# Turning query tiles 4 to 6 through DRAM and VectorE, with query chains one slot shorter

## The chip, the cores and the metric

The kernel runs on one core of a Trainium2 chip. The metric is the device time of one execution in microseconds (us). Before the change three runs gave 856.16, 856.25 and 856.46, median 856.25. The execution whose profile is shown took 856.38, and its span, from the first to the last instruction, is 854.6.

The engines are TensorE (PE, matrix products; its weight loads are PEld), VectorE (DVE), ScalarE (ACT), GpSimd (POOL) and SyncE (SP). SP issues most of the DMAs; "SPq" is its queue. Each engine takes its instructions in the order in which the program gives them.

## The reference

Linear attention feeds two MLPs with different activations:

```
q_s = exp(q - max(q, axis=-1));  q_s /= sum(q_s, axis=-1) + 1e-9
k_s = exp(k - max(k, axis=2));   k_s /= sum(k_s, axis=2) + 1e-9
kv  = einsum('bhsd,bhse->bhde', k_s, v)
x   = einsum('bhsd,bhde->bhse', q_s, kv)        # as rows: 2304 x 512
x   = elu(x @ w_in) @ w_out                     # 512 -> 2048 -> 512
out = mish(x @ w2_in) @ w2_out                  # 512 -> 2048 -> 512
```

There are 4 batches, 8 heads, 576 positions, head size 64, all in fp32. The four weights arrive as 64-bit floats and are decoded on the chip.

## The kernel before

The 2304 rows are 18 query tiles of 128 rows. The ELU layer takes them in five groups j of 4, 3, 4, 3 and 4 tiles (tiles 0 to 3, 4 to 6, 7 to 10, 11 to 13, 14 to 17). For each group it goes through 16 slots f, one for each 128 columns of the hidden layer. All products are split into a high and a low part, so a slot has 12 products `mm_h(f)` into the hidden layer and 12 products `mm_y(f-2)` out of it, each with up to 512 columns. The Mish layer comes after that and takes the rest of the time.

While the slots of group j run, the kernel prepares group j+1: the keys and values of the next batch (`kv_chain`) and the query tiles (`q_chain`). The steps are put into the slots by `at(j, f, where, fn, ...)`, and in every slot the lists "pre", "load", "mid", "pe", "post", "last" and "late" are run in that order around the slot's own work. Nothing reorders them: the place in the text is the place in each engine's queue. The first five slots of group 0 are an exception, there the list FIRST gives the order by names, and x0, x1, ... are the steps that `at` put there.

A query tile is loaded (`load_q`, on SP), its maxima are taken over each head (`q_max`, DVE) and subtracted (`q_less`; POOL for tiles 4 to 6, DVE for later ones), ACT takes the exponential (`q_exp`), DVE sums (`q_sum`, with two small instructions for the inverse), and the tile is scaled (`q_norm`, POOL or DVE). Then it has to be turned, so that the head's columns lie on the partitions:

- Tiles 4 to 6 are turned by TensorE: `q_turn` has four 128x128 transposes into PSUM, and ACT copies the result back (`q_turned`).
- Tiles 7 to 17 go out to DRAM (`q_out`), come back in four DMAs with their 32x32 blocks at the places of the turned tile (`q_in`), and DVE turns each block in place (`q_blocks`, one instruction).

At the end `q_x` multiplies with the kv matrices on TensorE, ACT copies the high part (`x_hi`), and DVE subtracts it for the low part (`x_lo`). With f the slot of the exponential, `q_x` of tiles 4, 5 and 6 stands in slots 10, 12 and 14 of group 0.

The query tiles lie in a pool with two buffers (tag "q", tiles 4, 5, 6, 7, 8, 10, ... take them in turn), so the load of a tile waits until `q_x` of the tile two before has read its buffer. One tile in each later group (o == 2) lies in one of the three key buffers instead (`load_q3`).

In every slot of group 0 two 512 KB weight pieces are decoded: ACT (`rebias`, slot f-1), two instructions of `decode_low` and two of `decode_join` on DVE (slot f, "pre"), a copy of the high part on ACT (`piece_hi`, "mid") and the low part on POOL (`piece_lo`). The slot's own vector work is `elu_join(f)` and, a slot later, `split_lo(f)`, which writes the tile gl that `mm_y(f)` needs from its second product on. Pieces that are no longer in the early buffers go through four "raw" buffers.

Of the kernel before, what the change touches and what calls it, by code (L numbers as in the profile page):

```python
# [8 lines left out]
F32 = mybir.dt.float32  # L9
F32R = mybir.dt.float32r  # L10
U32 = mybir.dt.uint32
# [5 lines left out]
P = 128  # L17
# [15 lines left out]
    lo0 en1 li3 2i4 1o2 ee2 ej1 2o1 my0 x2 x3 en2 pi4 ld1 2o2 ej2 li4 gh1 mh3 x4 x5 gh2 x6 bo3  # L33
    x7 1o3 1i5 mh4 gl1 bi5 2i5 po1 2o3 bi6 po2 1i6 lo1 gl2 x8 ee3 x9 po3 x10 x11 2i6 ee4
    my1 1o4 bo4 en3 2o4 x12 x13 lo2 x14 pi5 ej3 lo3 en4 x15 li5 x16 ej4 gh3 my2 ld3 pi6 mh5 ld2
    po4 li6 x17 ld4 lo4 gl3 x18
""".split()


# [1 line left out]
def attention_elu_mish(  # L41
# [15 lines left out]
    nc = tc.nc  # L57
    B, DM, S = kT.shape
# [3 lines left out]
    NHP = DM // P  # L62
# [6 lines left out]
    TILES = (4, 3, 4, 3, 4)  # L69
    NA = len(TILES)  # L70
    assert sum(TILES) * P == NT
    at0 = [sum(TILES[:j]) for j in range(NA)]
# [8 lines left out]
    NC = (S + P - 1) // P  # L81
# [6 lines left out]
    dram = ctx.enter_context(tc.tile_pool(name="dram", bufs=1, space=bass.MemoryType.DRAM))  # L88
# [25 lines left out]
    stage = att.enter_context(tc.tile_pool(name="stage", bufs=2))  # L114

    raw = {}
    w_hi, w_lo, split_t = {}, {}, {}
    w_src = {("i", 0): w1_in, ("o", 0): w1_out, ("i", 1): w2_in, ("o", 1): w2_out}  # L120

    def load_piece(kind, layer, f, t=None):
        w = w_src[kind, layer]
        if t is None:
            t = stage.tile([P, 512, 2], U32, tag="raw", name="raw", bufs=4)
        c = slice(f * P, (f + 1) * P)
        if kind == "i":
            nc.sync.dma_start(
                out=t.rearrange("p (k c) two -> p k (c two)", c=P),
                in_=w[:, c, :].rearrange("(k p) c two -> p k (c two)", p=P),  # L130
            )
        else:
            nc.sync.dma_start(out=t, in_=w[c, :, :])
        raw[kind, layer, f] = t
# [67 lines left out]
    ap = att.enter_context(tc.tile_pool(name="att", bufs=2))  # L202
# [3 lines left out]
    km_t, qm_t, kv_t, turn_t, x_t = {}, {}, {}, {}, {}  # L206
    k_t, v_t, q_t, rk_t, en_t = {}, {}, {}, {}, {}
# [25 lines left out]
    def load_q(i, t=None):  # L233
        if t is None:
            t = ap.tile([P, DM], F32, tag="q", name="q")
        nc.sync.dma_start(out=t, in_=q[i * P:(i + 1) * P, :])
        q_t[i] = t
# [76 lines left out]

    R = 32

    def q_out(i):
        d = dram.tile([P, DM], F32, name=f"turn_q{i}")
        nc.sync.dma_start(out=d, in_=q_t[i])
        turn_t[i] = d  # L320

    def q_in(i):

        d = turn_t.pop(i).rearrange("(a j) (h r i) -> r j h a i", j=R, r=P // R, i=R)
        for r in range(P // R):
            nc.sync.dma_start(
                out=q_t[i][r * R:(r + 1) * R, :].rearrange("j (h a i) -> j h a i", h=NHP, i=R),
                in_=d[r],
            )

    def q_blocks(i):
        nc.vector.transpose(out=q_t[i], in_=q_t[i])

    NH = DM // D

# [1 line left out]
        return q_t[i].rearrange("p (h d) -> p h d", d=D)  # L337

    def load_q3(i):
        t = ap.tile([P, NC, P], F32, tag="kT", name="kT", bufs=3)  # L340
        load_q(i, t.rearrange("p c e -> p (c e)")[:, 0:DM])

    def q_max(i):
        m = sp.tile([P, NH], F32, tag="qm", name="qm")
# [264 lines left out]
    for n, t in enumerate(("xhb", "xlb")):  # L609
        t = xpool.tile([P, KD * TILES[1] * P], F32, tag=t, name="early_x")  # L610
        for hp in (2 * n, 2 * n + 1):
            a = hp % 2 * NC * P
# [4 lines left out]
    def at(j, f, where, fn, *a):  # L617
        j, f = j + f // NF, f % NF
        beside.setdefault((j, f, where), []).append((fn, a))
# [5 lines left out]
    def kv_chain(j, f, b):  # L625
        for hp in range(NHP):

            s = f + 2 * hp
            if j or hp > 2:
                at(j, s - 2, "load", load_k, b, hp)  # L630
            if (b, hp) not in v_t:
                at(j, s + 2, "load", load_v, b, hp)
            at(j, s, "late", k_max, b, hp)
            at(j, s, "late", k_exp, b, hp)
            at(j, s + 2, "post", lambda b, hp: inverse(rk_t[b, hp]), b, hp)
            at(j, s + 3, "post", k_scale, b, hp)


            rest = s + 1 if j else s + 2
            if j and hp:  # L640
                at(j, s + 1, "pe", k_kv, b, hp - 1)
            at(j, rest, "pe", k_turn_rest, b, hp)
            at(j, rest, "pe", k_turned_rest, b, hp)
            if not j or hp == NHP - 1:
                at(j, s + 3, "pe", k_kv, b, hp)
            at(j, s + 1, "pe", k_turn, b, hp)
            at(j, s + 1, "pe", k_turned, b, hp)

    def q_chain(j, f, i, o):
        at(j, f - 2, "late", load_q3 if j and o == 2 else load_q, i)  # L650
        at(j, f - 1, "late", q_max, i)
        at(j, f - 1, "late", q_less, i, NORM[j])
        at(j, f, "mid", q_exp, i)
        at(j, f, "late", q_sum, i)
        at(j, f, "late", q_norm, i, NORM[j])
        for fn in (q_x, x_hi, x_lo):
            at(j, f + (5 if j else 2), "pe", fn, i)
        if j:
            at(j, f + 1, "late", q_out, i)
            at(j, f + 2, "late", q_in, i)  # L660
            at(j, f + 4, "post", q_blocks, i)
            return
        for fn in (q_turn, q_turned):
            at(j, f + 1, "pe", fn, i)


    turns = {-1: [("i", 0, 0), ("i", 0, 1)]}
# [8 lines left out]
    for j in range(NA - 1):  # L676
        if j + 1 < B:
            kv_chain(j, -1 if j else 0, j + 1)
        for o in range(TILES[j + 1]):
            q_chain(j, 9 - 3 * (TILES[j + 1] - 1 - o) if j else 8 + 2 * o, at0[j + 1] + o, o)  # L680

    for n in range(NF):
        j, s = 1 + n // 4, n % 4 * 4
        for key, s in ((("i", 1, n), s), (("o", 1, n), s + 2)):
            at(j, s - 2, "load", load_piece, *key)
            at(j, s - 1, "last", rebias, key)
            at(j, s, "pre", decode, key)
            at(j, s + 1, "mid", split_piece, *key)
# [4 lines left out]
    with tc.manual_schedule():  # L693
# [14 lines left out]
        def load_turn(f, which=(0, 1)):  # L708
            for n in which:
                key = turns[f][n]  # L710
                n += (f + 1) % 4 * 2
                t = early[4 + n // 2].bitcast(U32)[:, n % 2 * 1024:(n % 2 + 1) * 1024]
                load_piece(*key, t.rearrange("p (c two) -> p c two", two=2))
# [4 lines left out]
        def load_ahead(f):  # L718
            if f + 3 < RING:
                load_turn(f + 3)  # L720
            else:
                while later and sum(key in raw for key in late) < 4:
                    key = later.pop(0)
                    late.append(key)
                    load_piece(*key)

        late = []
# [73 lines left out]
        for key in [key for f in range(-1, AHEAD) for key in turns[f]]:  # L801
            n = f"{key[0]}{key[2]}"
# [10 lines left out]
        n = 0  # L813
# [27 lines left out]
        for s in range(AHEAD, len(slots) + LAG1):  # L841
            if s < len(slots):
                j, f = slots[s]
# [18 lines left out]
            if s >= LAG1:  # L862
                j, f = slots[s - LAG1]
# [9 lines left out]
        for s in range(len(slots) + LAG2):  # L873
            if s < len(slots):
                p, f = slots[s]
# [6 lines left out]
            if s >= LAG2:  # L882
                p, f = slots[s - LAG2]
# [41 lines left out]
```

## Time and profile before

| | |
|---|---|
| median of 3 runs | 856.25 us (856.16 to 856.46) |
| profiled execution | 856.38 us, span 854.6 us |
| PE busy | 843.7 us (99%) |
| DVE busy | 599.4 us (70%) |
| ACT busy | 451.1 us (53%) |
| POOL busy | 160.3 us (19%) |
| granted TensorE clock | 0.999 of full speed |
| DMA | 104.05 MB |

Busy time is the share of the span in which an engine had an instruction in work. The products of TensorE overlap, so the length shown for one is longer than the distance to the next; where a text speaks of the pace, it takes the distance of two starts. In a timeline the number in brackets is the idle time ahead of an instruction and what ended it.

### The profile page before, as it was taken

The page shows a single profiled execution, that of the slowest core. Times are in us where ns is not written, and L with a number is a line of the kernel's source. Part 1 is how long each engine was busy: PE and PEld are TensorE (multiplying, and loading weights), DVE is VectorE, ACT ScalarE, POOL GpSimd, SP SyncE. Part 2 cuts the span into 40 slices and gives each one's busy share as a digit, 9 for nine tenths or more (in the row PEclk, how much of TensorE's full clock was granted, in tenths as well). Part 3 has the DMA queues.
Part 4 walks back from the last instruction along what each step waited for, and adds up shares of the span by engine and source line. Part 5 has one row for each costly group of instructions (what it writes and reads, how often), then busy time and mean ns, then how long its engine had stood idle before and what let it go on. Part 6 is the DMA issues. An engine that isn't in the chain of part 4 may idle for free.

```text
span 854.6 us, 11819 instructions
## 1 busy us (share of the span) xinstructions
PE 843.7 (99%) x4364; PEld 728.6 (85%) x4364; DVE 599.4 (70%) x1051; ACT 451.1 (53%) x854; POOL 160.3 (19%) x210
## 2 busy tenths in 40 slices
PE   7999999999999999999999999999999999999998
PEld 5778889998888899988889998888888888888996
DVE  7899866665555577554446877777787777777776
ACT  7797757656554465554444444444444444444443
POOL 4366523233212242223332000000000000000000
PEclk9999999999999999999999999999999999999999
DMA  9791648673845196538876003000210021000101
GB/s 302 251 306 55 197 129 279 182 231 98 232 131 161 52 265 196 166 99 286 278 243 227 1 0 103 34 1 0 99 50 1 0 74 50 1 1 1 50 1 37
DMA packets 79865, 104.05 MB, mean 122 GB/s; under 512 B 27328, under 2 KB 56256, under 8 KB 77248
## 3 DMA queue, kind: packets, MB, share of 16 engines
q1 hardware_dynamic: 63536, 58.08, 22.8%
q0 software_dynamic: 16128, 45.09, 16.0%
q8 instruction: 34, 0.56, 0.3%
q14 instruction: 23, 0.19, 0.1%
q10 hardware_dynamic: 144, 0.13, 0.0%
HBM read 73.14 MB, written 30.15 MB: 121 GB/s over the span
## 4 chain that ended last, share of the span: by engine, by line
PE 95%; ACT 1%; issue 1%; POOL 1%; DVE 1%; DMA 0%; SPq 0%; POOLq 0%; ACTq 0%
PE h L428 45%; PE y L477 23%; PE y L565 15%; PE a L565 8%; PE a L388 2%; PE a L297 1%; PE a L263 1%; DMA q<-in_q_dram 0%; POOL wil L186 0%; PE a L280 0%; DVE qs L359 0%; ACT early L148 0%; PE a L374 0%; ACT woh L180 0%; POOL wol L186 0%
## 5 line engine op out<-in xcount | busy, mean ns | idle before, releaser
L443 DVE SCALAR_TENSOR_TENSOR e<-h,e 128x512 f32<-128x512 f32 (+1 forms) x80 | 50.9, 636 | 106.7 <-ACT e L439 106.2
L428 PE MATMUL h<-xha,wih 128*128 128x512 f32 (+1 forms) x328 | 125.0, 385 | 0.7 <-ACT xha L404 0.7
L428 PE MATMUL h<-xla,wih 128*128 128x512 f32 (+1 forms) x328 | 125.2, 385 | 0.4 <-DVE xla L408 0.4
L428 PE MATMUL h<-xha,wil 128*128 128x512 f32 (+1 forms) x328 | 125.2, 385 | 0.3 <-POOL wil L186 0.3
L533 ACT ACTIVATE r<-n,two 128x512 f32<-128x512 f32 (+1 forms) x80 | 54.6, 682 | 131.1 <-DVE n L529 131.1
L477 PE MATMUL y<-gh,wol 128*128 128x512 f32 (+1 forms) x320 | 120.1, 377 | 0.3 <-POOL wol L186 0.3
L477 PE MATMUL y<-gh,woh 128*128 128x512 f32 (+1 forms) x320 | 117.4, 368 | 0.0
L477 PE MATMUL y<-gl,woh 128*128 128x512 f32 (+1 forms) x320 | 117.2, 368 | 0.0
L435 ACT ACTIVATE e<-h 128x512 f32<-128x512 f32 (+1 forms) x80 | 44.5, 556 | 115.9 <-PE h L428 115.8
L428 PE MATMUL h<-xhb,wih 128*128 128x384 f32 (+1 forms) x304 | 104.7, 344 | 0.0
L428 PE MATMUL h<-xhb,wil 128*128 128x384 f32 (+1 forms) x304 | 104.6, 344 | 0.0
L428 PE MATMUL h<-xlb,wih 128*128 128x384 f32 (+1 forms) x304 | 104.4, 344 | 0.0
L186 POOL TENSOR_TENSOR lo<-raw,hi 128x512 fp32r<-128x512 f32 x32 | 43.9, 1372 | 229.9 <-ACT hi L180 144.8
L512 ACT ACTIVATE u<-h 128x512 f32<-128x512 f32 (+1 forms) x80 | 44.1, 551 | 72.1 <-PE h L428 72.1
L522 DVE TENSOR_SCALAR u<-u 128x512 f32<-128x512 f32 (+1 forms) x80 | 32.0, 400 | 64.9 <-ACT u L512 63.6
L565 PE MATMUL y<-woh,gl 128*128 128x512 f32 x192 | 75.2, 392 | 0.0
L565 PE MATMUL y<-woh,gh 128*128 128x512 f32 x192 | 75.1, 391 | 0.0
L565 PE MATMUL y<-wol,gh 128*128 128x512 f32 x192 | 74.7, 389 | 0.0
L461 DVE TENSOR_TENSOR gl<-e,gh 128x512 fp32r<-128x512 f32 (+1 forms) x80 | 52.4, 656 | 28.6 <-ACT gh L457 28.5
L428 PEld LDWEIGHTS h<-xha,wih 128*128 128x128 f32 x328 | 61.1, 188 | 13.2 <-ACT xha L404 0.9
L428 PEld LDWEIGHTS h<-xha,wil 128*128 128x128 f32 x328 | 61.1, 188 | 12.9 <-POOL wil L186 0.9
L457 ACT ACTIVATE gh<-e 128x512 fp32r<-128x512 f32 (+1 forms) x80 | 47.0, 588 | 47.3 <-PE y L477 39.3
(163 smaller groups left out, 1755.8 us busy)
## 6 DMA issues: line engine op xcount, KB each, us to landing
raw<-in_moe_w_out_dram SPq DMA_DIRECT2D x23, 512.0 KB, 4.9
raw<-in_moe_w_in_dram SPq DMA_DIRECT2D x21, 512.0 KB, 5.2
early<-in_moe_w_in_dram SPq DMA_DIRECT2D x11, 512.0 KB, 6.3
early<-in_moe_w_out_dram SPq DMA_DIRECT2D x9, 512.0 KB, 6.5
out_dram<-o SPq DMA_DIRECT2D x17, 256.0 KB, 2.0
w2ih<-hi POOLq DMA_DIRECT2D x16, 256.0 KB, 2.7
w2il<-lo POOLq DMA_DIRECT2D x16, 256.0 KB, 3.8
w2oh<-hi POOLq DMA_DIRECT2D x16, 256.0 KB, 3.3
```

Of the source, the lines that this page charges most:

```text
L186: nc.gpsimd.tensor_tensor(out=lo, in0=z, in1=hi.bitcast(F32), op=ALU.subtract)
L388: nc.tensor.matmul(out=ps[:, hp, t0:t1], lhsT=kvbd[b % 2][:, hp, :], rhs=u[:, hp, t0:t1], start=True, stop=True,)
L428: nc.tensor.matmul(out=h_t[f][:, c], lhsT=w[:, i, k * P:(k + 1) * P], rhs=x[k][:, c], start=(n == 0), stop=(n == 3 * KD - 1),)
L435: nc.scalar.activation(out=e, in_=h_t[f], func=AF.Exp)
L443: nc.vector.scalar_tensor_tensor(out=e, in0=h_t[f], scalar=0.0, in1=e, op0=ALU.max, op1=ALU.subtract)
L457: nc.scalar.activation(out=gh_t[f], in_=h_t[f], func=AF.Copy)
L461: nc.vector.tensor_tensor(out=gl_t[f], in0=h_t.pop(f), in1=gh_t[f].bitcast(F32), op=ALU.subtract)
L477: nc.tensor.matmul(out=y_t[e][:, 0:gh.shape[1]], lhsT=w[:, i, e * P:(e + 1) * P], rhs=x, start=(f == 0 and n == 0), stop=(f == NF - 1 and ...
L512: nc.scalar.activation(out=u, in_=h_t[f], func=AF.Exp)
L522: nc.vector.tensor_scalar(out=u, in0=u, scalar1=U_MAX, scalar2=None, op0=ALU.min)
L533: nc.scalar.activation(out=r, in_=n, func=AF.Ln, bias=two)
L565: nc.tensor.matmul(out=y_t[p, t], lhsT=x[:, c], rhs=w[:, i, :], start=(f == 0 and n == 0), stop=(f == NF - 1 and n == 2),)
```

## The change

Tiles 4 to 6 take the way through DRAM and VectorE that the later tiles take, and `q_turn` and `q_turned` are no longer used for them. All chains get one rule: `q_out` in slot f+1, `q_in` in f+2, `q_blocks` in f+3 and `q_x` in f+4, where f is the slot of the exponential. `q_x` stays in its slot for every tile. For tiles 4 to 6 that moves load, maxima, exponential, sum and scaling two slots ahead (f is 6, 8, 10 in place of 8, 10, 12), and for the later tiles all steps but the last two stand one slot later. The load of tile 4 falls into slot 4 and so becomes x19 at the end of FIRST.

Each raw buffer gets its own tag. The weights of the second layer use three of the four, and the fourth takes query tiles 9, 12 and 15, which no longer lie in key buffers. Tiles 4 to 6 stay in the pool with two buffers.

```diff
-    po4 li6 x17 ld4 lo4 gl3 x18
+    po4 li6 x17 ld4 lo4 gl3 x18 x19
...
-            t = stage.tile([P, 512, 2], U32, tag="raw", name="raw", bufs=4)
+            n = len(raw_use) % (4 if layer == 0 else 3)
+            raw_use.append(n)
+            t = stage.tile([P, 512, 2], U32, tag=f"raw{n}", name="raw", bufs=1)
...
-    def q_out(i):
-        d = dram.tile([P, DM], F32, name=f"turn_q{i}")
-        nc.sync.dma_start(out=d, in_=q_t[i])
-        turn_t[i] = d
+    def turn_out(key, t, n):
+        d = dram.tile([P, n * P], F32, name="turn_" + "_".join(map(str, key)))
+        nc.sync.dma_start(out=d, in_=t)
+        turn_t[key] = d
...
+    def q_out(i):
+        turn_out(("q", i), q_t[i], NHP)
+
+    def q_in(i):
+        turn_in(("q", i), q_t[i], NHP)
...
     def load_q3(i):
-        t = ap.tile([P, NC, P], F32, tag="kT", name="kT", bufs=3)
-        load_q(i, t.rearrange("p c e -> p (c e)")[:, 0:DM])
+        load_q(i, stage.tile([P, 4 * 512 // 2], F32, tag="raw3", name="q3", bufs=1)[:, 0:DM])
...
     def q_chain(j, f, i, o):
-        at(j, f - 2, "late", load_q3 if j and o == 2 else load_q, i)
+        at(j, f - 2, "late", load_q3 if j and i % 3 == 0 else load_q, i)
...
+        at(j, f + 1, "late", q_out, i)
+        at(j, f + 2, "late", q_in, i)
+        at(j, f + 3, "post", q_blocks, i)
         for fn in (q_x, x_hi, x_lo):
-            at(j, f + (5 if j else 2), "pe", fn, i)
-        if j:
-            at(j, f + 1, "late", q_out, i)
-            at(j, f + 2, "late", q_in, i)
-            at(j, f + 4, "post", q_blocks, i)
-            return
-        for fn in (q_turn, q_turned):
-            at(j, f + 1, "pe", fn, i)
+            at(j, f + 4, "pe", fn, i)
...
-            q_chain(j, 9 - 3 * (TILES[j + 1] - 1 - o) if j else 8 + 2 * o, at0[j + 1] + o, o)
+            q_chain(j, 10 - (3 if j else 2) * (TILES[j + 1] - 1 - o), at0[j + 1] + o, o)
```

The first place is the queue of SP in group 0, from the last raw loads ahead of the query tiles on. The tiles named q_798, q_921 and q_1056 before are query tiles 4, 5 and 6; after the change they are q_695, q_809 and q_938.

Before:

```order
L133 DMA raw_775<-in_moe_w_out_dram 128x1024
L236 DMA q_798<-in_q_dram 128x512
L236 DMA q_921<-in_q_dram 128x512
L128 DMA raw_1021<-in_moe_w_in_dram 128x4x256
L133 DMA raw_1023<-in_moe_w_out_dram 128x1024
L236 DMA q_1056<-in_q_dram 128x512
L128 DMA raw_1091<-in_moe_w_in_dram 128x4x256
```

The change, from the same raw load on:

```order
L135 DMA raw_780<-in_moe_w_out_dram 128x1024
L238 DMA q_809<-in_q_dram 128x512
L321 DMA turn_q_4_873<-q_695 128x512
L328 DMA q_695<-turn_q_4_873 32x16x32 x4
L238 DMA q_938<-in_q_dram 128x512
L321 DMA turn_q_5_997<-q_809 128x512
L130 DMA raw_1035<-in_moe_w_in_dram 128x4x256
L135 DMA raw_1037<-in_moe_w_out_dram 128x1024
L328 DMA q_809<-turn_q_5_997 32x16x32 x4
```

The load of tile 6 (q_938) now stands ahead of two raw loads (the pieces decoded in slot 11) that stood ahead of it before (raw_1021 and raw_1023), and ahead of the way out of tile 5.

The second place is DVE's queue around slots 9 to 11. The tiles raw_773 and raw_775 before, raw_778 and raw_780 after, are the pieces decoded in slot 10; gl_1019 and gl_1033 are the low part of slot 9, which `mm_y(9)` reads.

Before:

```order
L443 SCALAR_TENSOR_TENSOR e_956<-h_935,e_956 128x512
L345 TENSOR_REDUCE qm_985<-q_921 128x8
L154 TENSOR_SCALAR raw_773<-raw_773 128x512
L154 TENSOR_SCALAR raw_775<-raw_775 128x512
L161 SCALAR_TENSOR_TENSOR raw_773<-raw_773 128x512
L161 SCALAR_TENSOR_TENSOR raw_775<-raw_775 128x512
L461 TENSOR_TENSOR gl_1019<-e_956,gh_1013 128x512
L443 SCALAR_TENSOR_TENSOR e_1025<-h_1000,e_1025 128x512
L408 TENSOR_TENSOR xlb_1046<-a_1036,xhb_1045 128x4x128
L359 TENSOR_REDUCE qs_1051<-q_921 128x8
```

The change:

```order
L452 SCALAR_TENSOR_TENSOR e_973<-h_952,e_973 128x512
L333 STREAM_TRANSPOSE q_695<-q_695 128x512
L354 TENSOR_REDUCE qm_999<-q_938 128x8
L156 TENSOR_SCALAR raw_778<-raw_778 128x512
L156 TENSOR_SCALAR raw_780<-raw_780 128x512
L163 SCALAR_TENSOR_TENSOR raw_778<-raw_778 128x512
L163 SCALAR_TENSOR_TENSOR raw_780<-raw_780 128x512
L470 TENSOR_TENSOR gl_1033<-e_973,gh_1027 128x512
L452 SCALAR_TENSOR_TENSOR e_1039<-h_1014,e_1039 128x512
L417 TENSOR_TENSOR xlb_1060<-a_1050,xhb_1059 128x4x128
L368 TENSOR_REDUCE qs_1069<-q_938 128x8
```

In slot 9 the maxima of tile 6 stand where those of tile 5 stood, and the block turn of tile 4 stands ahead of them; in slot 10 the sums are those of tile 6.

The continuation of DVE's queue after the change, slots 11 and 12:

```order
L156 TENSOR_SCALAR raw_1035<-raw_1035 128x512
L156 TENSOR_SCALAR raw_1037<-raw_1037 128x512
L163 SCALAR_TENSOR_TENSOR raw_1035<-raw_1035 128x512
L163 SCALAR_TENSOR_TENSOR raw_1037<-raw_1037 128x512
L470 TENSOR_TENSOR gl_1105<-e_1039,gh_1099 128x512
L452 SCALAR_TENSOR_TENSOR e_1111<-h_1086,e_1111 128x512
L333 STREAM_TRANSPOSE q_809<-q_809 128x512
L156 TENSOR_SCALAR raw_1107<-raw_1107 128x512
```

The block turn of tile 5 (q_809) is the last vector instruction of slot 11; `q_x` of that tile is on TensorE in slot 12.

## Rows read from the trace of the kernel before

**Rows 1.** The page: busy time of PE; shares of the chain that ended last.

```profile
PE 843.7 (99%) x4364; PEld 728.6 (85%) x4364; DVE 599.4 (70%) x1051; ACT 451.1 (53%) x854; POOL 160.3 (19%) x210
...
PE 95%; ACT 1%; issue 1%; POOL 1%; DVE 1%; DMA 0%; SPq 0%; POOLq 0%; ACTq 0%
```

**Rows 2.** Timeline of PE: start us, length us, instruction and its number.

```profile
84.78 1.89 PE L388 MATMUL a<-q,kvbd 128*128 128x64 f32 x16
...
92.04 0.60 PE L374 MATMUL a<-ident,q 128*128 128x128 f32 x4
92.39 0.48 PE L477 MATMUL y<-gh,wol 128*128 128x512 f32 x1
92.71 0.40 PE L477 MATMUL y<-gl,woh 128*128 128x512 f32 x1
...
97.97 1.05 PE L388 MATMUL a<-q,kvbd 128*128 128x128 f32 x8
...
116.92 0.39 PE L477 MATMUL y<-gh,wol 128*128 128x512 f32 x1
117.14 0.39 PE L477 MATMUL y<-gl,woh 128*128 128x512 f32 x1
```

**Rows 3.** Waits of SP's queue: waiter, waited for, us in total, times, longest.

```profile
SPq L236 <- PE a L388: 2.7, 1, 2.7
```

**Rows 4.** Timeline of SP's queue, same columns as rows 2.

```profile
86.70 0.33 SPq L236 DMA_DIRECT2D q<-in_q_dram  x1
```

**Rows 5.** DMA issues of that load, then of four inward pieces: KB each, us to landing.

```profile
q<-in_q_dram SPq DMA_DIRECT2D x1, 256.0 KB, 3.2
...
q<-turn_q SPq DMA_DIRECT2D x4, 64.0 KB, 3.3
```

**Rows 6.** Line 236, all query loads.

```profile
DMA to landing us min/median/max: 2.8/4.4/9.5
```

**Rows 7.** Timeline of DVE in slots 9 to 11.

```profile
81.16 0.67 DVE L345 TENSOR_REDUCE qm<-q 128x8 f32<-128x512 f32 x1
81.75 0.74 DVE L154 TENSOR_SCALAR raw<-raw 128x512 uint32<-128x512 uint32 x2
82.50 3.18 DVE L161 SCALAR_TENSOR_TENSOR raw<-raw 128x512 uint32<-128x512 uint32 x2
85.60 0.68 DVE L461 TENSOR_TENSOR gl<-e,gh 128x512 fp32r<-128x512 f32 x1
86.27 0.69 DVE L443 SCALAR_TENSOR_TENSOR e<-h,e 128x512 f32<-128x512 f32 x1
88.39 0.69 DVE L408 TENSOR_TENSOR xlb<-a,xhb 128x512 fp32r<-128x512 f32 x1 [1.43 <-ACT xhb L404]
89.00 0.68 DVE L359 TENSOR_REDUCE qs<-q 128x8 f32<-128x512 f32 x1
...
90.04 1.56 DVE L154 TENSOR_SCALAR raw<-raw 128x512 uint32<-128x512 uint32 x2
91.52 1.28 DVE L161 SCALAR_TENSOR_TENSOR raw<-raw 128x512 uint32<-128x512 uint32 x2
92.72 0.68 DVE L461 TENSOR_TENSOR gl<-e,gh 128x512 fp32r<-128x512 f32 x1
```

**Rows 8.** Timeline of ACT in slot 10.

```profile
86.70 0.65 ACT L180 ACTIVATE woh<-raw 128x512 fp32r<-128x512 f32 x1
```

**Rows 9.** Line 332, the block turns of later tiles: ns min/median/max, first and last start.

```profile
L332 DVE STREAM_TRANSPOSE q<-q x8: 696/702/712, 144.4 to 354.4; 128x512 f32<-128x512 f32 x8
```

**Rows 10.** Timeline of POOL: subtracting and scaling of query tiles.

```profile
83.63 1.49 POOL L349 TENSOR_TENSOR q<-q,qm 128x512 f32<-128x512 f32 x1
...
90.27 1.05 POOL L364 TENSOR_TENSOR q<-q,qs 128x512 f32<-128x512 f32 x1 [0.74 <-ACT gh L457]
```

**Rows 11.** Timeline of SP's queue, four inward pieces of tile 10.

```profile
175.93 3.93 SPq L326 DMA_DIRECT2D q<-turn_q  x4
```

**Rows 12.** Timeline of DVE, the block turn of tile 10.

```profile
187.47 0.70 DVE L332 STREAM_TRANSPOSE q<-q 128x512 f32<-128x512 f32 x1
```

More of the change, by code (lines that the diff above doesn't have):

```diff
@@ L114, in attention_elu_mish @@
     stage = att.enter_context(tc.tile_pool(name="stage", bufs=2))
-    raw = {}
+    raw, raw_use = {}, []
     w_hi, w_lo, split_t = {}, {}, {}
@@ L315, in attention_elu_mish, with turn_in, turn_blocks @@
     R = 32
-    def q_out(i):
-        d = dram.tile([P, DM], F32, name=f"turn_q{i}")
-        nc.sync.dma_start(out=d, in_=q_t[i])
-        turn_t[i] = d
-    def q_in(i):
-        d = turn_t.pop(i).rearrange("(a j) (h r i) -> r j h a i", j=R, r=P // R, i=R)
+    def turn_out(key, t, n):
+        d = dram.tile([P, n * P], F32, name="turn_" + "_".join(map(str, key)))
+        nc.sync.dma_start(out=d, in_=t)
+        turn_t[key] = d
+    def turn_in(key, t, n):
+        d = turn_t.pop(key).rearrange("(a j) (c r i) -> r j c a i", j=R, r=P // R, i=R)
         for r in range(P // R):
             nc.sync.dma_start(
-                out=q_t[i][r * R:(r + 1) * R, :].rearrange("j (h a i) -> j h a i", h=NHP, i=R),
-                in_=d[r],
-            )
+                out=t[r * R:(r + 1) * R, :].rearrange("j (c a i) -> j c a i", c=n, i=R), in_=d[r]
+            )
+    def turn_blocks(t):
+        nc.vector.transpose(out=t, in_=t)
+    def q_out(i):
+        turn_out(("q", i), q_t[i], NHP)
+    def q_in(i):
+        turn_in(("q", i), q_t[i], NHP)
     def q_blocks(i):
-        nc.vector.transpose(out=q_t[i], in_=q_t[i])
+        turn_blocks(q_t[i])
     NH = DM // D
```

## The prediction

> **What bounds the kernel now.** I read the page's busy times and chain first. TensorE is busy for 843.7 of 854.6 us and has 95% of the chain that ended last; no other engine has over 1% [rows 1]. So an edit gains only what it takes off TensorE's queue, and it loses what makes TensorE wait. Then I read the timelines of group 0 around slots 9 to 12, engine by engine, to see when each operand of TensorE is finished and when it is wanted.
>
> On TensorE's timeline [rows 2] the reader is to see the three places on which the sum rests: q_x of tile 4 at 84.78, the turn of tile 5 at 92.04 with mm_y(9) behind it at 92.39, and q_x of tile 5 at 97.97. The queue has no gap there. On SP's the reader is to see that the load of tile 6 is already held up: it is issued at 86.70 [rows 4], and the waits of the queue put 2.7 us ahead of it down to line 388, which is q_x [rows 3]. This is the pool of two buffers: tile 6 takes the buffer of tile 4 and cannot come before q_x of tile 4 has read it. On DVE's timeline [rows 7] the reader is to see that the low part of slot 9 ends at 85.60 + 0.68 = 86.28, while mm_y(9) wants it with its second product at 92.71: VectorE is 6.4 us ahead, about one slot, and busy nearly all the time.
>
> **What is removed.** Three times four transposes. The turn of tile 5 takes 92.39 - 92.04 = 0.35 us of TensorE's time, and the product behind it has a distance of 92.71 - 92.39 = 0.32 to the next, where 117.14 - 116.92 = 0.22 to 0.23 is the pace without a turn [rows 2]. That is 0.44 per tile and 1.32 for three. The three copies back on ScalarE go too; ScalarE isn't in the chain, so I count nothing for them. The whole gain would be 1.32 us, and that is the most that can be had.
>
> **What is added, and where it is covered.** The block turns are one DVE instruction of 0.70 each [rows 9]. Load, maxima and sums of tiles 4 and 5 come two slots earlier; that is 1.6 us of DVE work (0.59 + 1.04, below) brought forward, and the 6.4 us of lead hide it. If that cover were gone the price would be those 1.6 us, but q_x of tile 4 at 84.78 only needs the turn that DVE makes behind elu_join(9), which ends where q_max begins before, at 81.16. So it is ready by 82.
>
> **The wait that is added.** The load of tile 6 now stands in slot 8 of SP's queue in place of slot 10, but it still waits for q_x of tile 4 in slot 10 of TensorE, so it is issued no earlier than before, less the one turn saved ahead of it: 86.70 - 0.44 = 86.26. It lands 3.2 us later [rows 5], at T = 89.46. What did move is who waits: the maxima of tile 6 are now in slot 9 of DVE's queue, behind elu_join(9) and the turn of tile 4. DVE gets there at about 81.9 and sits still until 89.5, 7.6 us, with all of slots 10 and 11 queued behind it: the decode of two pieces, the low part of slot 9, elu_join(10), x_lo(4), the sums of tile 6, the next decode, the low part of slot 10, elu_join(11) and the turn of tile 5. The lead was 6.4 us, so this does not fit.
>
> From T on, with durations as starts to next starts [rows 7]:
> - maxima 81.75 - 81.16 = 0.59; decode of two pieces with one POOL instruction beside it 92.72 - 90.04 = 2.68; the second join is ready at T + 3.27.
> - low part of slot 9, 0.67: T + 3.94 = 93.4. mm_y(9) wants it at 92.71 less two turns, 91.83. TensorE waits 1.6 us here.
> - elu_join(10), taken as 0.67 too: T + 4.61. But x_lo(4) needs x_hi(4), which on ScalarE comes behind the second high copy and the exponential of tile 6. Before, that copy starts at 86.70 [rows 8] and x_lo at 88.39, 1.69 later; so x_lo(4) starts at T + 3.27 + 1.69 = T + 4.96 and DVE waits 0.35.
> - x_lo 0.61, sums with inverse 90.04 - 89.00 = 1.04, decode 2.68, low part of slot 10 and elu_join(11) 0.67 each, turn of tile 5 0.70: in all T + 11.33 = 100.79.
>
> TensorE would come to q_x(5) at 97.97 - 0.88 + 1.57 = 98.66, so it waits another 2.1 us and starts it at 100.79 in place of 97.97: 2.82 late. The turn of tile 6 is still to be saved in the slot behind: 2.82 - 0.44 = **2.38 us slower**. Nothing gives this back later, since TensorE has no idle time that could take it up.
>
> What is behind this on the other queues I count at nothing. The way of tile 5 through DRAM waits for SP as well: out at 86.7, landed by about 90 at the pace of rows 5, its four inward pieces issued over 3.9 us [rows 11], the last landed 3.3 after issue, so by 97.1, which is before DVE gets to it at T + 10.63 = 100.1. The two raw loads behind tile 6's load come about 5 us later than before; they land by 93 and are decoded from T + 6.61 = 96.1 on. Tile 6 itself has two more slots until its q_x, and slots 12 and 13 of DVE have lost their maxima and sums.
>
> In the later groups all chains come one slot closer to q_blocks. The tightest tile that I found is tile 10: the last piece is issued at 175.93 + 3.93 and lands 3.3 later, at 183.2, and DVE turns it at 187.47 [rows 5, 11, 12], 4.3 us to spare. A slot of three tiles is 24 products at three quarters of 0.22, about 4.0 us as an estimate from rows 2. The cover just holds; if it fails, DVE waits 1 us there and TensorE has another slot before it wants the tile. The fourth raw buffer is taken from pieces that live four slots and come every two, so three hold them.
>
> Profile against median: 856.38 + 2.38 = 858.76 for an execution such as the profiled one; on the median of 856.25 it is 858.63. I predict **858.6**.
>
> **Bounds.** Two sizes are uncertain: the landing and the decode. Least landing of a query load 2.8 [rows 6], and both decodes without POOL beside them, 0.74 + 1.28 = 2.02 [rows 7]: T = 89.06, the work 11.33 - 1.32 = 10.01, q_x(5) at 99.07, 1.10 late, 0.66 us slower in all. Other end: landing 4.4, the median [rows 6], and both decodes as between 81.75 and 85.60, 3.85: T = 90.66, work 13.67, q_x(5) at 104.33, 5.9 us slower. I take 3.2, since it is this very load at this place, now with no raw load ahead of it in flight, and 2.68, since one POOL instruction of the query tiles falls on each decode (the subtraction, then the scaling).
>
> A rule of the Trainium skill makes the decode dearer. The row shows that the two low instructions take 1.56 at 90.04, with the POOL scaling of 1.05 beside them [rows 10], against 0.74 for the pair at 81.75: 0.82 more. "SBUF — State Buffer", section "Who interferes with whom", says that VectorE and GpSimd lock a port pair against each other for a whole instruction and the loser fully blocks. By that the first decode would take 2.02 + 1.49 and the second 2.02 + 1.05, together 1.22 more than I count, and the time would be 859.9. I go by the row.
>
> **Rivals.**
> 1. *VectorE catches up, no change in time.* The place is the same wait, with the price at the lower bound: 856.25 + 0.66 = 856.9. It decides for this if T plus the work stays under 100.12 (97.97 + 0.44 + 1.71, where 1.71 us is the 0.2% that a measurement of this kernel can just tell from no change). For it: 100.79 is only 0.7 above that point, and half a microsecond on the landing with one undisturbed decode would do. Against it: both POOL instructions come right behind the DVE instructions that release them and so fall on the decodes.
> 2. *The wait is hidden and the whole gain comes,* 856.25 - 1.32 = 854.9, not slower than before. This needs q_x(5) to find its tile by 97.09, so T + 11.33 = 97.09 and T = 85.8, before the buffer is free; with the cheapest work it still needs a landing in under 0.9 us. It is only possible if the buffer is free earlier than I read it. Against it is the wait on line 388 that the queue shows today.
> 3. *The backlog goes on.* With dear decodes DVE gets to q_x(5) at 104 and the pieces decoded in slots 11 and 12 become late too: 862.2 by the upper bound.
>
> **How the numbers follow.** The forecast (858.0 to 861) gets 0.55, rival 1 gets 0.27, rival 2 gets 0.11, rival 3 gets 0.07. The range for 8 in 10 goes from 855.6 to 861.0: it leaves out rival 2 and rival 3 and takes in rival 1 whole. The forecast's own range is 858.0 to 861.0. Slower by over 0.2% is the forecast and rival 3, 0.62. Within 0.2% are rival 1 and most of rival 2, whose 854.9 lies within 1.71 of 856.25: 0.33. Faster by over 0.2% is more than the turns cost in all and needs something that I haven't seen, a part of rival 2: 0.05.
>
> **What would show it.** In the profile of the changed kernel: the load of tile 6 on SP still issued at about 86.3, right behind q_x of tile 4; an idle time of 7 to 8 us on DVE ahead of the maxima of a query tile, ended by that load; a gap on TensorE of 1 to 2 us ahead of the second product of mm_y(9), put down to the low part; and one of about 2 us ahead of q_x(5), put down to the block turn on DVE. No other gap on TensorE should be new, in the later groups above all. I am wrong if the idle time on DVE isn't there (then the load wasn't held), or if it is there and TensorE has no gap (then VectorE had more lead than I count), or if gaps appear in groups 1 to 3.

## The result, and the profile after

The changed kernel takes **861.58 us** (median of 6 runs, 860.47 to 862.68) against 856.25 for the kernel before (6 runs of the same sitting): a ratio of 1.0060, 95% interval 1.0047 to 1.0073. It is slower by 5.3 us. The forecast was 858.6, with a range up to 861.0, so the sign was right, the size less than half, and the time outside the range. The six runs lie in two clumps, 860.5 to 861.2 and 862.0 to 862.7, three in each; that will matter below.

The profiled execution took 861.96 us (span 860.2). The page first, PE's busy time and the chain that ended last:

```profile
PE 844.8 (98%) x4352; PEld 728.1 (85%) x4352; DVE 597.5 (69%) x1054; ACT 449.8 (52%) x851; POOL 161.3 (19%) x210
...
PE 90%; DVE 2%; DMA 2%; ACT 2%; issue 2%; POOL 1%; SPq 1%; ACTq 0%; DVEq 0%; POOLq 0%
```

Against [rows 1], TensorE has twelve matmuls fewer (the turns of three tiles) and is yet busy 1.1 us longer, and its share of the chain has fallen from 95 to 90%: there are new waits, and some products run slower.

**Group 0.** The timeline of SP's queue (start, length, line, what is moved), at the load of tile 6 and behind it:

```profile
86.12 0.35 SPq L238 DMA_DIRECT2D q<-in_q_dram  x1
86.97 0.33 SPq L321 DMA_DIRECT2D turn_q<-q  x1
...
89.67 2.76 SPq L328 DMA_DIRECT2D q<-turn_q  x4
```

The load goes out at 86.12, against 86.70 before [rows 4]. The 0.58 us are what TensorE has gained by then, so against `q_x` of tile 4 the buffer is no sooner free. DVE's timeline shows who waits for it (in square brackets the idle time ahead of an instruction and what ended it):

```profile
80.96 0.70 DVE L333 STREAM_TRANSPOSE q<-q 128x512 f32<-128x512 f32 x1
88.94 0.69 DVE L354 TENSOR_REDUCE qm<-q 128x8 f32<-128x512 f32 x1 [7.28 <-DMA q<-in_q_dram]
89.54 1.60 DVE L156 TENSOR_SCALAR raw<-raw 128x512 uint32<-128x512 uint32 x2
91.06 1.28 DVE L163 SCALAR_TENSOR_TENSOR raw<-raw 128x512 uint32<-128x512 uint32 x2
92.27 0.68 DVE L470 TENSOR_TENSOR gl<-e,gh 128x512 fp32r<-128x512 f32 x1
...
94.09 0.69 DVE L417 TENSOR_TENSOR xlb<-a,xhb 128x512 fp32r<-128x512 f32 x1 [0.54 <-ACT xhb L413]
...
95.73 1.57 DVE L156 TENSOR_SCALAR raw<-raw 128x512 uint32<-128x512 uint32 x2
97.21 1.28 DVE L163 SCALAR_TENSOR_TENSOR raw<-raw 128x512 uint32<-128x512 uint32 x2
98.42 0.68 DVE L470 TENSOR_TENSOR gl<-e,gh 128x512 fp32r<-128x512 f32 x1
...
99.62 0.70 DVE L333 STREAM_TRANSPOSE q<-q 128x512 f32<-128x512 f32 x1
```

Before, the maxima of a query tile stood at 81.16 with no wait [rows 7]. Now DVE turns tile 4, stands still for 7.28 us until tile 6 has landed, and goes through the queue behind it without another long pause. The low part of slot 9 comes at 92.27, the turn of tile 5 at 99.62. TensorE's timeline, at the two places that want these, and the products behind:

```profile
93.00 0.50 PE L486 MATMUL y<-gl,woh 128*128 128x512 f32 x1 [1.16 <-DVE gl L470]
...
100.37 1.31 PE L397 MATMUL a<-q,kvbd 128*128 128x128 f32 x8 [1.82 <-DVE q L333]
101.33 0.78 PE L486 MATMUL y<-gh,wol 128*128 128x512 f32 x1
101.91 0.63 PE L486 MATMUL y<-gl,woh 128*128 128x512 f32 x1
102.33 0.63 PE L486 MATMUL y<-gh,woh 128*128 128x512 f32 x1
...
104.79 0.39 PE L486 MATMUL y<-gh,woh 128*128 128x512 f32 x1
105.02 0.39 PE L486 MATMUL y<-gh,wol 128*128 128x512 f32 x1
```

Two gaps of 1.16 and 1.82 us are new. And behind the second the products follow each other at 0.42 us (102.33 less 101.91) in place of the 0.23 of [rows 2], until about 104.5; then they are at 0.23 again. The table by stretches says why (length; busy time of PE, PEld, DVE, ACT, POOL with counts; granted clock; DMA share; GB/s):

```profile
94.00:100.30 6.30, 4.55 (x20) 3.39 (x19) 6.15 (x12) 4.76 (x9) 4.05 (x5) 1.00 0.81 218
100.30:105.30 5.00, 4.93 (x19) 4.13 (x20) 4.87 (x8) 3.96 (x7) 3.28 (x3) 0.66 0.70 194
105.30:112.00 6.70, 6.70 (x31) 5.55 (x30) 5.22 (x8) 5.00 (x9) 2.63 (x4) 1.00 0.90 257
```

In the middle stretch the granted clock is 0.66 on average: TensorE was at its lower level of 1.2 GHz for most of it, and it is at 2.4 GHz in the stretches before and after.

**The later groups.** At the start of group 1, the four inward pieces of tile 7 on SP's queue, their landing (KB each, median us), and the turn that waits for them:

```profile
139.49 5.07 SPq L328 DMA_DIRECT2D q<-turn_q  x4
```

```profile
q<-turn_q SPq DMA_DIRECT2D x4, 64.0 KB, 7.3
```

```profile
150.53 0.71 DVE L333 STREAM_TRANSPOSE q<-q 128x512 f32<-128x512 f32 x1 [3.46 <-DMA q<-turn_q]
```

The kernel before, the same tile on SP's queue and on DVE:

```profile
127.55 2.71 SPq L326 DMA_DIRECT2D q<-turn_q  x4
```

```profile
144.39 0.70 DVE L332 STREAM_TRANSPOSE q<-q 128x512 f32<-128x512 f32 x1
```

There the pieces landed in 3.3 us and lay ready for some ten. Now they stand behind the loads of a query tile, of values and of keys; they are issued 11.9 us later (3.3 of it the lag of group 0), take twice as long to issue and 7.3 us to land, and DVE waits 3.46 us for them. The stretches of their issue, before and then after, in the table's columns (the last is GB/s):

```profile
127.55:130.30 2.75, 2.75 (x15) 2.28 (x14) 1.43 (x4) 2.31 (x5) 1.21 (x1) 1.00 0.98 294
```

```profile
139.50:144.60 5.10, 5.10 (x32) 5.10 (x31) 3.01 (x8) 3.54 (x8) 1.73 (x2) 1.00 1.10 413
```

The DMA engines had work throughout in both. After the change 1.60 of the 2.14 MB of that stretch are POOL's transfers, on a queue of their own; before there are none of these.

At the border of groups 2 and 3, DVE's timeline with the sums and scaling of tile 14, and PE's behind it:

```profile
305.34 0.69 DVE L368 TENSOR_REDUCE qs<-q 128x8 f32<-128x512 f32 x1
306.06 1.22 DVE L254 TENSOR_SCALAR qs<-qs 128x8 f32<-128x8 f32 x1
...
308.17 2.48 DVE L496 TENSOR_TENSOR xla<-y,xha 128x512 fp32r<-128x512 f32 x4
```

```profile
308.91 0.44 PE L486 MATMUL y<-gh,wol 128*128 128x384 f32 x1 [0.33 <-DVE xla L496]
```

The four subtractions at the group's end (line 496) free the banks of `y`. The sums now stand ahead of them for 308.17 - 305.34 = 2.83 us, and the first `mm_y` of the new group waits for its banks.

**Where the time went.** TensorE's lag (start of the same product after, less before; the turns have no partner) tells it place by place:

| place | lag behind it | step |
|---|---|---|
| ahead of the first turn's place | -0.16 | -0.16 |
| two turns saved, up to `mm_y(9)` | -0.94 | -0.78 |
| wait for the low part of slot 9 | +0.40 | +1.34 |
| wait for the turn of tile 5 | +2.55 | +2.15 |
| products at the lower clock | +4.11 | +1.56 |
| third turn saved | +3.3 | -0.8 |
| tile 7 (`q_x`, then the keys' turns) | +4.24 | +0.9 |
| tile 14 at the groups' border | +5.09 | +0.85 |
| last product | +5.09 | 0 |

From the last product to the end of the span it is 5.0 us after and 4.5 before. The last output is issued 1.36 us after the last product starts in both, so the other 0.5 us lies behind that issue. In the profiles below, the kernels of experiment 4 and of experiment 5 with tile 7 have 4.5, all others 4.9 to 5.0. What makes the difference isn't shown.

### The profile page after: what moved, and what is told of

Read it like the earlier page. It is cut to its first block, busy times and chain, and to the rows that moved or that the text cites. A ratio compares the mean times of both kernels' runs of the same rounds, so it can differ in the third digit from the quotient of the medians.

```text
span 860.2 us, 11837 instructions
## 1 busy us (share of the span) xinstructions
PE 844.8 (98%) x4352; PEld 728.1 (85%) x4352; DVE 597.5 (69%) x1054; ACT 449.8 (52%) x851; POOL 161.3 (19%) x210
## 4 chain that ended last, share of the span: by engine, by line
PE 90%; DVE 2%; DMA 2%; ACT 2%; issue 2%; POOL 1%; SPq 1%; ACTq 0%; DVEq 0%; POOLq 0%
PE h L437 43%; PE y L486 21%; PE y L574 15%; PE a L574 8%; PE a L397 2%; DMA q<-turn_q 1%; DMA q<-in_q_dram 1%; PE a L299 1%; PE a L265 1%; DMA turn_q<-q 0%; SPq L328 0%; DVE qs L368 0%; POOL wil L188 0%; DVE qs L254 0%; ACT kT L250 0%
## 5 line engine op out<-in xcount | busy, mean ns | idle before, releaser
L437 PEld LDWEIGHTS h<-xla,wih 128*128 128x128 f32 x328 | 61.2, 188 | 12.6 <-DVE xla L417 0.6
```

The source lines that it names most:

```text
L437: nc.tensor.matmul(out=h_t[f][:, c], lhsT=w[:, i, k * P:(k + 1) * P], rhs=x[k][:, c], start=(n == 0), stop=(n == 3 * KD - 1),)
```

## Experiments

The question was which of four things made up the 5.3 us: the wait for tile 6's buffer, the lower clock behind it, the shorter chains of the later groups, and the raw buffers, three in place of four. Each is undone by itself. The times are medians; the kernel before had 856.38 in the first sitting, 856.36 and 856.39 in the next two.

**1. Tile 6 in a buffer of its own.** One of the three key buffers, which is free then:

```diff
+    def load_q6(i):
+        t = ap.tile([P, NC, P], F32, tag="kT", name="kT", bufs=3)
+        load_q(i, t.rearrange("p c e -> p (c e)")[:, 0:DM])
...
-        at(j, f - 2, "late", load_q3 if j and i % 3 == 0 else load_q, i)
+        at(j, f - 2, "late", load_q6 if i == 6 else load_q3 if j and i % 3 == 0 else load_q, i)
```

> The changed kernel, except that query tile 6 lies in a key buffer that is free by then, so its load needn't wait for q_x of tile 4. Theory A (the load of tile 6 holds up VectorE, and with it TensorE in slots 9 to 12): the 7.3 us of idle time on VectorE and TensorE's gaps ahead of mm_y(9) and q_x(5) are gone, the stretch at a lower clock behind them too, and group 0 ends 1.3 us earlier than in the kernel before; what the later groups lost stays (0.7 + 0.3 at tile 7, 0.8 at tile 14), so about 856.7 us. Rival B (the raw loads that now come later, or the added block turns on VectorE, hold up TensorE): the gaps stay and the time stays at 860 or above.

Measured: 857.05 us (856.28 to 857.64, 11 runs), ratio 1.0005 (0.9996 to 1.0014), where theory A had 856.7. DVE's timeline at the place of the 7.28 us wait:

```profile
81.07 0.69 DVE L333 STREAM_TRANSPOSE q<-q 128x512 f32<-128x512 f32 x1
81.69 0.63 DVE L358 TENSOR_REDUCE qm<-kT 128x8 f32<-128x512 f32 x1
```

The maxima follow the turn at once, there is no gap on TensorE between 84 and 106 us, and the granted clock is 1.00 throughout. One buffer takes back 4.5 of the 5.3 us, the lower clock with it.

**2. The later chains a slot longer again, alone.** The chains of groups 1 to 4 as before the change, tile 6 still waiting:

```diff
-        at(j, f + 3, "post", q_blocks, i)
+        late = 1 if j else 0
+        at(j, f + 3 + late, "post", q_blocks, i)
...
-            at(j, f + 4, "pe", fn, i)
+            at(j, f + 4 + late, "pe", fn, i)
...
-            q_chain(j, 10 - (3 if j else 2) * (TILES[j + 1] - 1 - o), at0[j + 1] + o, o)
+            q_chain(j, (9 if j else 10) - (3 if j else 2) * (TILES[j + 1] - 1 - o), at0[j + 1] + o, o)
```

> The changed kernel with only the chains of the later groups put back to the kernel before; tile 6 is still held up. If the shorter chain costs 1.8 us in the later groups: 861.6 - 1.8 = 859.8 us, with the gaps in slots 9 to 12 unchanged. If it costs nothing and group 0 has it all: 861.6.

Measured: 859.91 us (858.71 to 860.27, 5 runs), ratio 1.0032 (1.0019 to 1.0045): 1.7 us of the 5.3. It shows a second thing. Its profiled execution is the one at 858.71, and its stretch of 100.3 to 105.3 us reads

```profile
100.30:105.30 5.00, 4.76 (x25) 4.11 (x26) 4.93 (x8) 3.94 (x7) 3.23 (x4) 1.00 0.63 176
```

Both gaps are there, 1.12 and 1.82 us, but TensorE kept 2.4 GHz behind them in this execution. It was at the lower clock elsewhere, early in the kernel, and as the fastest of its five runs it shows no loss by that:

```profile
11.00:16.00 5.00, 4.53 (x56) 3.57 (x58) 4.28 (x11) 4.29 (x12) 0.30 (x1) 0.66 1.11 315
```

So a run's mean clock (0.997 here) doesn't tell whether the products behind the gaps were slow. Three of the five runs lie 1.2 to 1.6 us above it, the same distance as between the two clumps of the changed kernel.

**3. Both edits.**

> As e1_own_buffer, and the chains of the later groups stand where the kernel before had them (load to q_in one slot earlier, five slots from the exponential to q_x). Theory A with the later groups' loss put down to the shorter chain: only the saved turns are left, 856.25 - 1.3 = 854.9 us. Rival C (the later groups lose by the buffers, the three raw buffers or the key buffers, and not by the chain): as e1_own_buffer, about 856.7.

Measured: 855.10 us (854.87 to 855.48, 11 runs), ratio 0.9982 (0.9973 to 0.9991). This is **faster than both kernels**: 1.28 us under the kernel before, where the three turns were put at 1.32. With both waits gone the gain of the turns is there. That the two figures meet is in part luck: TensorE's lag goes from +0.35 us ahead of the first turn's place to -1.31 behind the third's, so the turns gave 1.66 on its queue, and 0.4 of that goes again behind the last product.

**4. Three raw buffers alone.** The kernel before, with only this part of the change, and query tiles 9, 12 and 15 in the fourth buffer. (Before, the tiles in a key buffer were 9, 13 and 16, those with o == 2.)

```diff
-            t = stage.tile([P, 512, 2], U32, tag="raw", name="raw", bufs=4)
+            n = len(raw_use) % (4 if layer == 0 else 3)
+            raw_use.append(n)
+            t = stage.tile([P, 512, 2], U32, tag=f"raw{n}", name="raw", bufs=1)
...
-        at(j, f - 2, "late", load_q3 if j and o == 2 else load_q, i)
+        at(j, f - 2, "late", load_q3 if j and i % 3 == 0 else load_q, i)
```

> The kernel before with only the buffers changed: three raw buffers for the second layer's weights, the fourth for query tiles 9, 12 and 15. Theory A: no change, 856.2 to 856.5 us. Rival C (the buffers cost the later groups their time): 857 to 858.

Measured: 856.15 us (855.93 to 856.84, 11 runs), ratio 0.9995 (0.9987 to 1.0004). Taking the fourth raw buffer away costs nothing, as the prediction had it.

**5. Tiles 7 and 14 apart.** Both start from experiment 1 (857.05 us) and lengthen the chain of one tile only: `late = 1 if i == 14 else 0` with the start of that chain a slot earlier, and the same for tile 7.

> The kernel with tile 6 in a buffer of its own (857.05 us), and the chain of tile 14 alone a slot longer again, as in the kernel before. Theory G: of the 1.95 us that the longer chains of all later tiles gave, 0.8 belong to tile 14, whose sums and scaling stand in DVE's queue ahead of the subtractions of the group's end and so keep the y banks; so 856.2 us, and no wait of mm_y for the subtraction of line 500 at 304 us. Rival: the 0.8 us at the group's boundary come from the general backlog of the shorter chains, and tile 14 alone gives nothing: 857.0.

> The kernel with tile 6 in a buffer of its own (857.05 us), and the chain of tile 7 alone a slot longer again. Theory G: 1.15 us belong to tile 7, whose inward pieces don't land before DVE comes to its block turn (3.7 us of idle time on DVE ahead of it, then 0.75 us of TensorE ahead of q_x of tile 7 and the rest at the turns of keys behind it); so 855.9 us, and no gap ahead of q_x of tile 7 at about 146 us. Rival: VectorE is late there for another reason (its own work of the group), and the gap only moves to the next thing that TensorE wants: 856.7 or more.

Measured: 856.26 us for tile 14 (855.57 to 857.91, 11 runs; ratio 1.0000, 0.9991 to 1.0009) and 855.69 for tile 7 (855.37 to 856.09, 11 runs; ratio 0.9992, 0.9983 to 1.0001). So they give 0.79 and 1.36 us; 2.15 together, where all later tiles gave 857.05 - 855.10 = 1.95. The two together take all that the later tiles cost, so for the others nothing is left. With tile 14 lengthened DVE's subtractions are back ahead of its sums:

```profile
301.90 2.48 DVE L500 TENSOR_TENSOR xla<-y,xha 128x512 fp32r<-128x512 f32 x4 [1.04 <-ACT xha L499]
```

And with tile 7 lengthened, its pieces on SP's queue and its turn on DVE:

```profile
126.01 2.62 SPq L328 DMA_DIRECT2D q<-turn_q  x4
```

```profile
141.97 0.70 DVE L333 STREAM_TRANSPOSE q<-q 128x512 f32<-128x512 f32 x1
```

The pieces go out ahead of the loads of the group again, and DVE waits no more for them.

**6. TensorE kept busy in the second gap.** The changed kernel, with products that nobody reads ahead of `q_x` of tile 5, first four, then two:

```diff
-        ps = att_psum().rearrange("p (c t) -> p c t", t=P)
+        ps = att_psum()
+        if i == 5:
+            for n in range(4):
+                nc.tensor.matmul(
+                    out=ps, lhsT=ident, rhs=kvbd[0].rearrange("p c e -> p (c e)"),
+                    start=True, stop=True,
+                )
+        ps = ps.rearrange("p (c t) -> p c t", t=P)
```

> The changed kernel with one addition: right ahead of q_x of tile 5, TensorE computes four extra products of 512 columns (ident by key/value columns) into the PSUM buffer that q_x then overwrites, some 0.43 us each as an estimate from the turns' rows, so about 1.7 of the 1.82 us in which it waits for the block turn of tile 5. No result depends on them. Theory D: the products behind q_x of tile 5 run at half pace (granted clock 0.66 in 100.3 to 105.3 us) because TensorE stood still twice ahead of them; with the second gap filled it keeps its upper level of 2.4 GHz, no stretch of 100 to 106 us is under 0.9, and the kernel takes 860.6 in all of its runs, as the changed kernel does in those of its runs that keep the clock (860.5 to 861.2). Theory E: the lower clock has nothing to do with the gap ahead of q_x of tile 5; about half of the runs still have it, and the runs lie between 860.5 and 862.7 with a median near 861.6. Theory F: the extra products push out later work, and the time rises by up to 1.7 us, to 863.3.

Measured: 861.99 us (861.3 to 862.31, 5 runs), ratio 1.0065 (1.0052 to 1.0077). The 860.6 of theory D is missed, but the trial was mis-sized: I had put a product at 0.43 us, and PE's timeline shows

```profile
98.56 3.60 PE L394 MATMUL a<-kvbd,ident 128*128 128x512 f32 x8
101.99 1.05 PE L404 MATMUL a<-q,kvbd 128*128 128x128 f32 x8
```

The four take 101.99 - 98.56 = 3.43 us, 0.86 each, so 1.6 more than the gap. Less these 1.6 the time is 860.4, and the granted clock behind them is 1.00. All five runs have a mean clock of 1.000, where the three upper runs of the changed kernel have 0.997. That speaks for theory D, but a time that needs a subtraction isn't enough. Hence the same with two products, in the changed kernel and in that of experiment 2:

> The changed kernel with two extra products of 512 columns ahead of q_x of tile 5 in place of four: the run with four showed 3.43 us for them (98.56 to 101.99), 0.86 each, so two take 1.72 of the 1.82 us in which TensorE waits for the block turn of tile 5, and cost nothing by themselves. Theory D: with the second gap filled TensorE keeps 2.4 GHz behind it in every run, and every run lies where the changed kernel's runs with a clock of 0.999 to 1.0 lie, 860.5 to 861.2; median 860.7. Theory E: the lower clock comes and goes for another reason; some runs have it, with a mean clock of 0.997 and 862.0 to 862.7 us, as three of the changed kernel's six have. Theory E2: filling the gap costs as much as it gives, since the wait for the block turn moves to the next piece; median 861.6, all runs near it.

> The same two products in the kernel with the chains of the later tiles a slot longer (859.91 us; its runs lay at 858.7 and at 859.9 to 860.3). Theory D: every run at the lower of these, 858.7 (858.4 to 859.1). Theory E: runs at both, median 859.5 or more. Theory E2: all at 859.9.

Measured: 860.68 us (859.78 to 860.92, 5 runs; ratio 1.0048, 1.0036 to 1.0061) and 858.84 (858.63 to 859.39, 7 runs; ratio 1.0030, 1.0019 to 1.0041). PE's timeline and the stretch behind, of the first:

```profile
98.64 1.88 PE L394 MATMUL a<-kvbd,ident 128*128 128x512 f32 x4
100.64 1.16 PE L404 MATMUL a<-q,kvbd 128*128 128x128 f32 x8
101.56 0.48 PE L493 MATMUL y<-gh,wol 128*128 128x512 f32 x1
101.88 0.39 PE L493 MATMUL y<-gl,woh 128*128 128x512 f32 x1
102.11 0.40 PE L493 MATMUL y<-gh,woh 128*128 128x512 f32 x1
```

```profile
100.30:105.30 5.00, 4.88 (x25) 4.01 (x25) 4.35 (x8) 3.95 (x7) 2.92 (x3) 1.00 0.71 197
```

`q_x` of tile 5 starts no earlier than in the changed kernel (100.64, 100.37), yet the products behind it are at 0.23. With work in the gap, all 5 runs of the first kernel lie in or under the lower clump of the changed kernel, and all 7 of the second (859.39 is its highest) under the three upper runs of experiment 2 (859.91 and more); without it, 6 of 11 lay in the upper clumps. One run of the first kernel has a mean clock of 0.997, but at 860.68 us it shows no loss. So it is the standstill that lowers the clock behind it, in about half of the runs, at 1.5 us a time; one trace shows this, the other runs are told by their times. That TensorE's clock has the two levels 1.2 and 2.4 GHz, and that the chip judges its activity on a beat that doesn't start with the kernel, is what the Trainium skill says ("TensorE: Matmul & The Clock Gate", section "What's actually happening"); that runs of one program differ agrees with it. No run here shows what decides whether a run falls, or whether the second gap would do it without the first.

## Why the prediction was right in sign and wrong in size

The sum now closes. The mechanism that was forecast, by itself (no lower clock, later chains long), is the second kernel of experiment 6: **858.84 us, where the prediction said 858.6**. That it comes so near is in part luck: in its profile TensorE's last product starts 1.86 us late, where 2.38 were forecast, and 0.4 more lies behind it, for which the sum had no term. The changed kernel adds 860.68 - 858.84 = 1.84 us for tiles 7 and 14, and 861.58 - 860.68 = 0.90 us for the clock, as a median over runs that have it and runs that don't.

*What held.* "This is the pool of two buffers": the load was issued at 86.12 (forecast 86.26). It landed in 2.8 us and not 3.2, so T was 88.94 (89.46), and DVE sat still for 7.28 us (7.6). From T the low part of slot 9 came at T + 3.33 (T + 3.27), the turn of tile 5 ended at T + 11.30, when the next instruction starts at 100.24 (T + 11.33). TensorE waited 1.34 us by its lag (1.57) and 2.15 (2.13). Two turns saved 0.78 by the lag up to `mm_y(9)` (0.88). The third saved 0.7 to 0.8 and not 0.44, an error in the kernel's favour. The prediction had taken all three from the rows of tile 5; the kernel before shows for tile 6

```profile
104.11 0.39 PE L428 MATMUL h<-xha,wih 128*128 128x512 f32 x1
104.57 0.66 PE L374 MATMUL a<-ident,q 128*128 128x128 f32 x4
104.98 0.47 PE L477 MATMUL y<-gh,wol 128*128 128x512 f32 x1
105.30 0.39 PE L477 MATMUL y<-gl,woh 128*128 128x512 f32 x1
```

that is 1.19 us from the last `mm_h` to the second product behind the turn, where two distances of 0.23 would stand without it: 0.73. The sizes around the two waits fit nearly one for one since every duration came from a row of the same place.

*The decode.* The two came to 92.27 - 89.54 = 2.73 and 98.42 - 95.73 = 2.69 us, against the row's 2.68. POOL's instructions beside them:

```profile
89.76 1.10 POOL L358 TENSOR_TENSOR q<-q,qm 128x512 f32<-128x512 f32 x1 [6.87 <-DVE qm L354]
...
95.95 1.05 POOL L373 TENSOR_TENSOR q<-q,qs 128x512 f32<-128x512 f32 x1 [0.56 <-ACT raw L150]
```

They lie on the decodes, as the prediction said. The rule of the Trainium skill ("SBUF — State Buffer", section "Who interferes with whom") had been priced as the whole of a POOL instruction added to 2.02, 3.5 and 3.1 us; the rows measure 2.7. The rule isn't refuted by that, only its pricing: in each case the pair on DVE starts 0.22 us ahead of POOL (89.54, 89.76) and ends 0.3 us behind POOL's end. The pair comes to its end only when POOL is done, but the part of POOL's time that falls on an instruction already in work costs nothing. So the pair takes 1.60, which is 0.86 more than the 0.74 of [rows 7], not 1.10 more; and the subtraction itself took 1.10, where [rows 10] have 1.49. The pair of [rows 7] wasn't free of POOL either, as the prediction took it to be:

```profile
81.76 1.92 POOL L186 TENSOR_TENSOR wol<-raw,woh 128x512 fp32r<-128x512 f32 x1
```

There POOL came second by 0.01 us and was the slower one (its like at 88.21 took 1.32), while the pair kept its 0.74.

*What failed, first: "In the later groups ... the cover just holds".* The step named tile 10 as the tightest tile that was found, with a slot of 4.0 us against 4.3 to spare. Tile 10 and its like did hold. The tiles at a group's border did not, and they hadn't been looked at: a slot taken off the chain is counted in the queue's order, not in microseconds. On SP's queue at the start of group 1 that slot holds the loads of a whole group, so that the pieces of tile 7 went out 8.6 us later than the lag explains, and beside POOL's transfers; there their landing went from 3.3 to 7.3. (Which of the two, queue or traffic, lengthened it was not tried apart.) On DVE the slot of tile 14 moved its sums from ahead of the last products of a group to between these and the subtractions that free the banks of the next. The prediction's own sentence, that gaps in groups 1 to 3 would show it wrong, is what the profile shows. Priced at nothing, measured 1.84 us.

*Second: a gap was priced as its length.* The forecast's two gaps came true, but in half of the runs the second costs 1.5 us more, since TensorE falls to its lower clock behind it. As a median over all runs that is 0.90 us. No term of the sum held that, nor a bound. The upper bound (862.2) came near for another reason: dear decodes, which the rows refute, so rival 3 isn't what happened although its time is near.

*The rivals.* Rival 1 (VectorE catches up) needed T plus the work under 100.12, and it was 100.24: it missed by 0.12 us, with the faster landing that the prediction named as half of its condition. Rival 2 (the buffer free earlier) is refuted by 86.12; what it would have given appears once the tile has its own buffer and the later chains their slot, 855.10 against 854.9.

## What to carry to other kernels

Ask of a transfer that is moved earlier in a queue when its buffer is freed, not when it is issued: an in-order engine that waits for it holds all that stands behind, and one more buffer gave back 4.5 us here. A "slot" is not a time: when all chains are shortened by one, look at each queue at the borders of the loops, where a slot holds the loads and the hand-over of a whole group. And put a price on a gap of TensorE beyond its length, since the products behind it may run at half pace.

## What the runs showed of the hardware

- Two gaps of 1.2 and 1.8 us, with 5.5 us of work between them, were enough to bring TensorE's granted clock to 0.66 over the next 5 us in about half of the runs (6 of 11, one by its trace and the rest by their times), at 1.5 us each; with the second gap filled by two products, in none of 12 by their times.
- A product of 512 columns with fp32 operands took 0.86 us, where those of fp32r take 0.23: the trace counts it as two matmuls (four products, x8).
- Four inward pieces of 64 KB took 2.7 us to issue and 3.3 to land behind a query load and a raw load, and 5.1 and 7.3 behind the loads at a group's start, with 1.6 MB of POOL's transfers beside them.
- A pair of uint32 TENSOR_SCALAR on VectorE, 0.76 us with no GpSimd instruction beside it (at 30.90 in the kernel before), took 1.57 to 1.60 with a GpSimd TENSOR_TENSOR of 1.05 to 1.10 that started 0.22 us behind it, and ended 0.3 us after that.
